# Moving one small product and its softmax away from the DMA that feeds it: a Fourier mix with eight experts on one core

## The chip, the cores and the metric

The kernel runs on one core of a Trainium2 chip. What is compared is the device time of one launch in microseconds (us). The engines are named as in the profile: PE is the matrix engine, PEld its weight loads, DVE the vector engine, ACT the scalar engine, POOL the general engine, and SP the engine whose queue issues most of the DMAs. Each works through its instructions in a fixed order and waits at an instruction until what it needs has been signalled.

## The reference, cut to what matters

The input has 8 batches of 2496 rows of 256 numbers. Each batch is transformed along its rows, mixed by two weight matrices in the frequency domain, cut by a soft threshold and transformed back. Each resulting row goes to one of 8 experts, and an expert keeps only its 80 rows of highest gate.

```python
X = np.fft.rfft(x, axis=1)
Yr = Xr @ w_r - Xi @ w_i + b_r
Yi = Xr @ w_i + Xi @ w_r + b_i
Yr = np.sign(Yr) * np.maximum(np.abs(Yr) - lam, 0.0)   # Yi alike
y = np.fft.irfft(Y, n=2496, axis=1)
...
logits = y @ w_gate                      # 19968 x 8
expert_idx = np.argmax(logits, axis=1)
probs = softmax(logits); gate_w = probs[n, expert_idx[n]]
for e in range(8):
    keep = the 80 rows of expert e with the highest gate_w
    out[keep] = gate_w[keep, None] * (np.maximum(y[keep] @ w1[e], 0) @ w2[e])
```

## The kernel before, in words

The main loop has 16 steps, two for each batch: step i works on half of batch i//2, and its first and last stages already serve the neighbouring steps. `stageA` (product at L296) transforms the input along one factor of the length and stores the result `zd` to memory; `loadZ` brings it back as `z`, half a step or more ahead of its use; `stageB` (product at L344, copies at L351 to L355) transforms along the other factor; `mixes` (products at L418, L460 to L470) mixes and thresholds; `stageTs` and `stageD` (L585 to L600) turn the result, and `stageHB` (L615, L640 to L652) makes the rows `hd` that the experts read later. Zero rows of the output (`out<-zero`, L268) are stored a few at a time all along.

A batch's gate is computed beside this. The logits come out of `stageD` in the small tile `Gs`. `stageE1a` sums them, `stageE1b` (L731 to L747) transforms them back along one factor and stores the result to memory as `gd` in two DMAs (L743, L744), then reads it back in the other order as `gr` in two DMAs (L747), which wait for the stores. `stageE2` is the product that turns the gate back along the second factor (L791) and behind it the softmax: ten instructions of DVE (L799 to L813) and one exponential of ACT (L801). `stageE3` transposes the result (L819) and copies it to `sall` (L824). From `sall` the best of each list are chosen: `level1(0)` and `level2` for the first four batches, as small operations that `doP` issues a few at a time (`pump`), the other four batches behind the loop.

Batch b's `stageE1b` is called in step 2b+3, its `stageE2` at the end of that step, and its `stageE3` in step 2b+4. All products write to tiles of a pool of four buffers in PSUM (`psum()`): a product waits until the engine that reads the buffer's former content is done with it. `stageE2` keeps its buffer from the product to the last of the ten instructions, which read and write in it. The order on each engine is made by a scheduler from the order of the calls, the dependences and its own costs; SP issues its DMAs in that order too, and a DMA that has to wait holds up those behind it.

The calls of step i that matter here, in the order in which they stand:

```python
doC(0, 0); doB(); doC(0, 1); doA(); doC(0, 2); doHB(); doB()
doP(); doW(...)
if pend3: stageE3(*pend3.pop())          # in step 10 then pump = level1(0), level2
pend = [(p[0], stageE1b(*p)) for p in pend]
...
if pend and not end:
    p = pend.pop(); sc = stageE2(*p)
doP(); doW(...)
```

Of the kernel before, what the change touches and what calls it, by code (L numbers as in the profile page):

```python
# [10 lines left out]
F32 = mybir.dt.float32  # L11
# [11 lines left out]
CAP = 80  # L23
# [109 lines left out]
def fourier_mix_then_moe(ctx, tc, x, w_r, w_i, b_r, b_i, wg, w1, w2, t1, t2, vq, v3, v0, v1f, vt, sg, cst, cb, out):  # L133
    nc = tc.nc
# [4 lines left out]
    ek = ctx.enter_context(tc.tile_pool(name="ek", bufs=1))  # L139
# [10 lines left out]
    gd = [dr.tile([39, 64, 8], F32, name=f"gd{b}") for b in range(B)]  # L150
# [219 lines left out]
    hops = []  # L370
# [36 lines left out]
    def doS():  # L407
        while totals:
            totals.pop(0)()
# [316 lines left out]
    def stageE1b(b, gp):  # L726
        pt = psum()

        for t, (tab, k) in enumerate(((vqs, 2), (vis, 8), (vqs, 14))):
            for v, h in ((0, 0), (0, 1), (1, 0)):  # L730
                nc.tensor.matmul(pt[:, 48 * t:48 * t + 48], tab[:, v], gp[:, h, k:k + 6, :], start=(v + h == 0), stop=(v == 1))  # L731
        special(pt[:64, 512:536], gp)
        gh = ek.tile([128, 21, 8], F32, name="gh", bufs=1)
        gu = ek.tile([128, 48], F32, name="gdif")
        sc = 2.0 / S / XS
        g = float(np.sqrt(0.75))
        at = lambda a: gh[:, 6 * a:6 * a + 6].rearrange("p k e -> p (k e)")
        nc.scalar.activation(at(0), pt[:, 0:48], AF.Copy, scale=sc)
        nc.scalar.activation(gh[:64, 18:21], pt[:64, 512:536].rearrange("p (a e) -> p a e", a=3), AF.Copy, scale=sc)
        nc.vector.scalar_tensor_tensor(gu, pt[:, 96:144], -1.5 * sc, at(0), op0=ALU.mult, op1=ALU.add)  # L740
        for a, f in ((1, g), (2, -g)):
            nc.vector.scalar_tensor_tensor(at(a), pt[:, 48:96], f * sc, gu, op0=ALU.mult, op1=ALU.add)
        nc.sync.dma_start(gd[b][0:21].rearrange("q n e -> n q e"), gh[0:64])  # L743
        nc.sync.dma_start(gd[b][21:39].rearrange("q n e -> n q e"), gh[64:128, 0:18])  # L744
        gr = ek.tile([78, 32, 8], F32, name="gr", bufs=1)
        for h in range(2):
            hops.append(nc.sync.dma_start(gr[39 * h:39 * h + 39], gd[b][:, 32 * h:32 * h + 32, :]))  # L747
        return gr

    def stageE1c(b, gp):  # L750

# [64 lines left out]
    def stageE3(b, sc):  # L816
        pt = psum()
        for h in range(2):
            nc.tensor.transpose(pt[:, 128 * h:128 * h + 78], sc[:, 4 * h:4 * h + 4].rearrange("p e n -> p (e n)"), ident[:78, :78])  # L819
        o, i = sall[:, :, b], pt[:, :256].rearrange("p (h f) -> p h f", h=2)[:, :, :78]  # L820
        if b >= B - 2:
            nc.vector.tensor_copy(o, i)
        else:
            nc.scalar.activation(o, i, AF.Copy)  # L824
# [84 lines left out]
    def doW(n=1):  # L909
        for _ in range(n):  # L910
            if wq:
                _, step, load = wq.pop(0)
                load()
                step()

                for w in wq[:2] if ahead else ():
                    w[2]()
# [54 lines left out]
    def level1(g):  # L972

        cv = None if g else const.tile([128, 2, 8], F32, name=f"cv{g}")
        ci = const.tile([128, 2, 8], U32, name=f"ci{g}")
        g0, n = 4 * g, 4
        if g:

            pt = psum()
            cv = pt[:, 512:528].rearrange("p (h r) -> p h r", h=2)  # L980
        for h in range(2):
            row = sall[:, h, g0:g0 + n].rearrange("p b r -> p (b r)")
            nc.vector.max(out=cv[:, h], in_=row)
            nc.vector.max_index(out=ci[:, h], in_max=cv[:, h], in_values=row)
        if g == 0:
            nc.sync.dma_start(cvd.rearrange("(h j) n r -> (j n) h r", h=2), cv)
        else:

            cm = VT[0].rearrange("p (h n r) -> p h n r", h=2, n=32)
            for h in range(2):  # L990
                vops.append(nc.vector.tensor_tensor(cm[:, h], mod32.unsqueeze(2).to_broadcast([128, 32, 8]), cv[:, h].unsqueeze(1).to_broadcast([128, 32, 8]), op=ALU.mult))
                hops.append(nc.tensor.matmul(pt[:8, 0:256], div32[:, h], cm[:, h].rearrange("p n r -> p (n r)"), start=(h == 0), stop=(h == 1)))
            Vs.append(pt[:8, 0:512])
        tok = const.tile([128, 2, 8, 4], I32, name="tokb" if g == 1 else "tok")
        nc.vector.memset(tok, 0)
        k = []
        new = lambda dt: const.tile([128, 2, 8], dt, name=f"tk{len(k)}", tag=f"tk{k.append(0) or len(k)}")
        inp = (lambda dt: pt[:, 512 + 16 * len(k):528 + 16 * len(k)].rearrange("p (q h r) -> p (q h) r", h=2, q=k.append(0) or 1)) if g else new
        k.append(0)
        if g:  # L1000
            tokens(new, inp, 8, tok, ci, g0, n, R1, 8, 0)
            return []
        return tokens(new, inp, 8, tok, ci, g0, n, 0, 8, 0, True)
# [409 lines left out]
    def doA(n=1):  # L1413
        for _ in range(n):
            if not Aq:
                if not xls:
                    preX()
                if xls:
                    (b, c), xt = xls.pop(0)
                    Aq.extend([(b, 2 * c, xt), (b, 2 * c + 1, xt)])  # L1420
            if Aq:
                stageA(*Aq.pop(0))
            if not Aq:
                preX()
# [3 lines left out]
    def doP(n=1):  # L1428
        for _ in range(n):
            if pump:  # L1430
                with tc.issue_after(dvs[-1].ins):
                    pump.pop(0)()

    def doHB(n=1):
        for _ in range(n):
            if HBq:
                stageHB(*HBq.pop(0))
# [56 lines left out]
    prev = None  # L1494
    Gs = None
    pend = []
    pend3 = []
    pend3 = []
    pump = []
    for i in range(len(steps)):  # L1500
        b, ch = steps[i]
        end = i + 1 == len(steps)
# [18 lines left out]
        def doB():  # L1521
            doS()
            if Bs:
                stageB(*Bs.pop(0))

        RR = {}

        parts = {}

        def doC(eh, k):  # L1530
            if k == 0:
                R = wkr.tile([128, 14 * 128], F32, name="R", bufs=2)
                RR[eh] = R.rearrange("p (c l k) -> p c l k", c=2, k=64) if b < B - 1 else R[:, :11 * 128].rearrange("p (l c k) -> p l c k", c=2, k=64)
                if b < B - 1:
                    parts[eh] = mixes(ch, XT, RR[eh], eh)
                    if i == 0 and eh == 0:
                        parts[eh][3](1)
                        parts[eh][3](0)
            fast = end or (i == 14 and eh == 1)
            if b < B - 1:  # L1540
                parts[eh][k]()
            else:
                stageC(ch, XT, RR[eh], eh, k, fast)
            doS()
            if k == (2 if b < B - 1 else 1) and not end:
                YT[eh] = wka.tile([128, 2, 11, 2, 64], F16, name="YT", bufs=3)
                if b < B - 1:
                    stageTs(ch, RR[eh], YT, eh)
                else:
                    stageT(ch, RR[eh], YT, eh, copy=False)  # L1550
                    if eh:
                        stageT2(ch, RR[1], YT, 1, False)
                        with tc.issue_after(yts[-1].ins):
                            stageT2(ch, RR[0], YT, 0, False)

        if end:
# [23 lines left out]
            with tc.high_priority():  # L1580
                gp = stageG0(b, prev[2])
                p = pend.pop()
# [7 lines left out]
        if i == 1:  # L1590
            doC(0, 0); doC(0, 1); doC(0, 2); doA()
        elif b < B - 1:
            doC(0, 0); doB(); doC(0, 1); doA(); doC(0, 2); doHB(); doB()
        else:
            doC(0, 0); doB(); doA(); doHB(); doB()
        if i == 13:
            late_load()
        doP(); doW({12: 1, 13: 1, 14: 1}.get(i, 1))
        if pend3:
            stageE3(*pend3.pop())  # L1600
            if i == 10:
                pump = level1(0)
                bg = level2("b", CAP, 8)
        if i == 11:
            late_ops, pump = pump, list(bg[3])
            while late_ops:
# [9 lines left out]
            doC(0, 1); doD(); doHB(); doB(); doD()  # L1616
        if i == 0:
            doA(3)
        doP(); doW({12: 1, 13: 1, 14: 1}.get(i, 1))
        if i > 0:  # L1620
            zfill()
# [9 lines left out]
        doP(); doW({12: 1, 13: 1, 14: 1}.get(i, 1))  # L1631
        if prev:
            HBq.extend((pb, YO, pch, x) for x in ((-1, 1, 0, 2) if pch == 0 else (1, 0, 2)))
        sc = None
        if i in (11, 12, 13):
            doP()
        if i > 0:
# [8 lines left out]
            flush()  # L1646
        if pend and not end:
            p = pend.pop()
            sc = stageE2(*p)
        doP(); doW({12: 1, 13: 1, 14: 1}.get(i, 1))  # L1650
        if sc is not None:
            pend3 = [(p[0], sc)]
        if i == 0:
            znext = loadZ(*steps[2])
            hold.clear()
# [38 lines left out]
    with tc.high_priority():  # L1694
        gr = back()
        sc = stageE2(b, gr, True)
# [101 lines left out]
```

## Time and profile before

| | us |
|---|---|
| median of 3 runs | 612.48 (609.36 to 618.34) |
| the profiled execution's own time | 609.48 |
| its span, first to last instruction | 607.7 |
| PE busy | 533.2 (88% of the span) |
| DVE busy | 403.9 (66%) |
| ACT busy | 352.5 (58%) |
| POOL busy | 377.5 (62%) |
| DMA, mean over the span | 219 GB/s |

The main loop takes about the first 490 us and the experts the rest. In a timeline a row gives the start, the duration and the instruction; brackets tell how long the engine had stood idle before it and what ended the wait. A matrix product of 32-bit numbers is recorded as several instructions. The clock of a stretch is the share of full speed that was granted to PE: 1.00 is 2.4 GHz, 0.50 is 1.2 GHz.

### The profile page before, as it was taken

The numbers are of one execution on the slowest core, as the hardware profiler recorded it, in microseconds if no ns is written. First come the engines' busy times: TensorE is split into PE (matmuls) and PEld (weight loads), VectorE is DVE, ScalarE is ACT, GpSimd is POOL, SyncE is SP. The second block draws the span as 40 slices with busy tenths as digits, with TensorE's granted clock in tenths as the row PEclk, the third lists the DMA queues.
The fourth block names the chain that finished last, engine by engine and source line by source line (L and its number), as shares of the span: only waits on it lengthen the run. The fifth ranks groups of instructions, "written<-read, shape, count | busy, mean of one in ns | idle before, by whom it ended". The sixth has DMA issues, their size and how long they took to land. (4 is left out here: it accounts for less than half of the span.)

```text
span 607.7 us, 11933 instructions
## 1 busy us (share of the span) xinstructions
PE 533.2 (88%) x4408; PEld 382.1 (63%) x4408; DVE 403.9 (66%) x829; ACT 352.5 (58%) x558; POOL 377.5 (62%) x306
## 2 busy tenths in 40 slices
PE   8978889999699999989997989997789997979592
PEld 3864566767376767766674657774666574539591
DVE  3145437767566888666765698897696777947650
ACT  1135557668366767765665557775675538543561
POOL 2012685778456777765687368698885259756671
PEclk9979999999799999999998899999799998998897
DMA  7898899798889878978898889798584545878730
GB/s 167 270 211 199 249 246 262 227 283 214 212 215 290 254 199 250 254 211 232 246 249 222 219 232 289 194 307 234 142 254 118 170 157 163 268 239 271 275 90 23
DMA packets 95869, 133.85 MB, mean 220 GB/s; under 512 B 27094, under 2 KB 78573, under 8 KB 94167
## 3 DMA queue, kind: packets, MB, share of 16 engines
q1 hardware_dynamic: 88124, 116.04, 69.1%
q0 software_dynamic: 2128, 9.25, 4.6%
q10 hardware_dynamic: 5553, 7.73, 4.4%
q8 instruction: 37, 0.61, 0.4%
q14 instruction: 27, 0.22, 0.1%
HBM read 70.36 MB, written 62.63 MB: 219 GB/s over the span
## 5 line engine op out<-in xcount | busy, mean ns | idle before, releaser
L418 PEld LDWEIGHTS <-WM 128*128 128x128 f16 x1008 | 99.1, 100 | 59.5 <-issue 14.4
L418 PE MATMUL ps<-XT,WM 128*128 128x337 f16 (+1 forms) x672 | 99.3, 297 | 7.4 <-DVE Gs L600 2.6
L529 POOL TENSOR_TENSOR YT<-R,YT 128x1408 f16<-128x1408 f32 (+1 forms) x28 | 73.4, 2620 | 46.5 <-ACT YT L528 46.5
L344 PE MATMUL ps<-t2s,z 128*128 128x128 f32 x640 | 86.6, 285 | 7.6 <-DMA z<-zd 4.7
L344 PEld LDWEIGHTS ps<-t2s,z 128*128 128x128 f32 x640 | 80.7, 199 | 11.6 <-DVE WM L213 4.0
L296 PE MATMUL ps<-xt,t1f 117*117 117x512 f32 (+1 forms) x170 | 80.2, 595 | 5.9 <-DMA xt<-in_x 2.3
L354 DVE TENSOR_TENSOR tp<-ps,tp 128x320 f32<-128x320 f32 (+2 forms) x56 | 27.3, 487 | 66.2 <-ACT XT L352 61.2
L470 POOL TENSOR_TENSOR R<-R,tp 128x674 f32<-128x674 f32 (+1 forms) x28 | 42.4, 1514 | 46.1 <-ACT R L468 46.1
L355 DVE TENSOR_TENSOR XT<-ps,XT 128x768 f16<-128x768 f32 (+1 forms) x64 | 52.1, 814 | 5.4 <-ACT XT L352 5.4
L640 PE MATMUL ps<-YO,vqs 128*128 128x512 f16 (+1 forms) x252 | 49.8, 339 | 3.4 <-DVE R L466 1.9
L597 DVE TENSOR_TENSOR YO<-ps,YO 128x768 f16<-128x768 f32 (+1 forms) x50 | 45.4, 908 | 7.1 <-ACT YO L596 6.9
L464 POOL TENSOR_TENSOR R<-R,sgs 128x576 f32<-128x576 f32 x28 | 36.2, 1294 | 19.6 <-DVE R L462 10.2
L296 PEld LDWEIGHTS ps<-xt,t1f 117*117 117x117 f32 (+1 forms) x170 | 27.9, 178 | 31.7 <-issue 22.2
L352 ACT ACTIVATE XT<-ps 128x768 f16<-128x768 f32 (+1 forms) x64 | 44.8, 700 | 2.8 <-PE ps L344 2.8
L585 PE MATMUL ps<-wgi,YT 128*128 128x144 f16 (+1 forms) x302 | 42.7, 227 | 2.1 <-DVE R L462 0.6
L596 ACT ACTIVATE YO<-ps 128x768 f16<-128x768 f32 (+1 forms) x50 | 38.4, 778 | 9.6 <-PE ps L586 9.3
L528 ACT ACTIVATE YT<-R 128x1408 f16<-128x1408 f32 (+1 forms) x28 | 35.6, 1270 | 13.2 <-POOL R L525 13.2
L640 PEld LDWEIGHTS <-vqs 128*128 128x128 f16 x252 | 25.2, 101 | 27.1 <-issue 10.6
L586 PE MATMUL ps<-wgi,YT 128*128 128x136 f16 (+1 forms) x302 | 41.5, 222 | 0.0
L351 ACT ACTIVATE tp<-ps 128x320 f32<-128x320 f32 (+2 forms) x56 | 24.3, 433 | 28.8 <-PE ps L344 24.8
L467 ACT ACTIVATE tp<-R,lams 128x674 f32<-128x674 f32 (+1 forms) x28 | 22.8, 815 | 19.4 <-DVE R L466 18.4
L311 ACT ACTIVATE zs<-ps 117x1024 f32<-117x1024 f32 (+1 forms) x23 | 21.8, 950 | 19.6 <-PE ps L296 15.2
(299 smaller groups left out, 1150.3 us busy)
## 6 DMA issues: line engine op xcount, KB each, us to landing
out<-zero SPq DMA_DIRECT2D x48, 384.0 KB
hd<-hs SPq DMA_DIRECT2D x96, 192.0 KB
zd<-zs SPq DMA_DIRECT2D x108, 156.0 KB
xt<-in_x SPq DMA_DIRECT2D x42, 312.0 KB
z<-zd SPq DMA_DIRECT2D x32, 320.0 KB
z<-zd SPq DMA_DIRECT2D x16, 384.0 KB
pair<-in_moe_w SPq DMA_DIRECT2D x11, 512.0 KB
z<-zd SPq DMA_DIRECT2D x16, 256.0 KB
```

Source lines behind the costliest of these rows:

```text
L296: nc.tensor.matmul(pt[:K, 512 * j:512 * j + 512], t1f[:K, :K], xv[:, 2 * j:2 * j + 2], start=True, stop=True)
L344: nc.tensor.matmul(o, z2[u][:, l, 128 * dh:128 * dh + 128], t2s[:, cl, :], start=True, stop=True)
L352: nc.scalar.activation(ov(0), pv, AF.Copy)
L355: nc.vector.tensor_tensor(ov(1), pv, ov(0), op=ALU.subtract)
L418: nc.tensor.matmul(pt[:, 512 * k:512 * k + n], WM[:, dh, m, wh, 128 * eh:128 * eh + 128], x(dh, xh)[:, c0 + n * k:c0 + n * k + n], start=( ...
L470: nc.gpsimd.tensor_tensor(fv(Rf), fv(Rf), fv(t), op=ALU.subtract)
L529: nc.gpsimd.tensor_tensor(yv(1), rv, yv(0), op=ALU.subtract)
L585: nc.tensor.matmul(pt[:, off:off + w], yt(0), wgi[:, eh, 0:w], start=True, stop=False)
L586: nc.tensor.matmul(pt[:, off:off + w - w % 128 // 2], yt(1), wgi[:, eh, 0:w - w % 128 // 2], start=False, stop=True)
L596: dev.append(nc.scalar.activation(yoh, yy, AF.Copy))
L597: dvs.append(nc.vector.tensor_tensor(yol, yy, yoh, op=ALU.subtract))
L640: nc.tensor.matmul(o, tab[:, v], yo(h), start=(i == 0), stop=(i == 2))
```

## The change

For batches 0 to 2 `stageE1b` now stores `gd` and hands back a function `turn`, which issues the two loads of `gr`; it is called at the end of the step, where `stageE2` was called before. `stageE2` itself is called in the next step: for batches 0 to 2 behind the first third, where `stageE3` stood, and for batch 3 (whose loads stay with `stageE1b`) behind the first `doB` of step 10. `stageE3` follows at the end of the step for batches 0 to 2 and in the middle of step 10 for batch 3; `level1(0)` and `level2` follow it there, and step 10 gets one more `doP`. Batches 4 to 7 keep their places.

```diff
-        gr = ek.tile([78, 32, 8], F32, name="gr", bufs=1)
-        for h in range(2):
-            hops.append(nc.sync.dma_start(gr[39 * h:39 * h + 39], gd[b][:, 32 * h:32 * h + 32, :]))
-        return gr
+
+        def turn():
+            gr = ek.tile([78, 32, 8], F32, name="gr", bufs=1)
+            for h in range(2):
+                hops.append(nc.sync.dma_start(gr[39 * h:39 * h + 39], gd[b][:, 32 * h:32 * h + 32, :]))
+            return gr
+        return turn if b < 3 else turn()
...
+        def doE(at):
+            if pend2 and at == (1 if i < 10 else 0 if i == 10 else 2):
+                p = pend2.pop()
+                pend3.append((p[0], stageE2(*p)))
+
+        def doE3():
+            nonlocal pump, bg
+            if pend3:
+                stageE3(*pend3.pop())
+                if i == 10:
+                    pump = level1(0)
+                    bg = level2("b", CAP, 8)
...
-            doC(0, 0); doB(); doC(0, 1); doA(); doC(0, 2); doHB(); doB()
+            doC(0, 0); doB(); doE(0); doC(0, 1); doA(); doC(0, 2); doHB(); doB()
...
-        if pend3:
-            stageE3(*pend3.pop())
-            if i == 10:
-                pump = level1(0)
-                bg = level2("b", CAP, 8)
+        doE(1)
+        if i > 10:
+            doE3()
...
+        if i == 10:
+            doE3()
...
             p = pend.pop()
-            sc = stageE2(*p)
+            pend2.append((p[0], p[1]() if p[0] < 3 else p[1]))
+        doE(2)
         doP(); doW({12: 1, 13: 1, 14: 1}.get(i, 1))
-        if sc is not None:
-            pend3 = [(p[0], sc)]
+        if i < 10:
+            doE3()
+        elif i == 10:
+            doP()
```

The scheduler moves few other instructions, and the same instructions stand in both programs. Lines of the changed kernel behind the first edit are higher: the product L791 is L794 there, the softmax L802 to L816, the transposes L822, the loads of `gr` L749.

On PE, the product of batch 0 stood behind the last product of `stageHB` for the first two classes (L615) and ahead of the next one (L640):

```order
L615 LDWEIGHTS v0s
L615 MATMUL ps<-YO,v0s 64x256
L791 MATMUL ps<-gr,v1fs 78x256
L640 LDWEIGHTS vqs
L640 MATMUL ps<-YO,vqs 128x512
```

It now stands behind the second `stageB` of the next step (`t2s`, `z`), ahead of the first `stageD` (`wgi`, `YT`):

```order
L344 MATMUL ps<-t2s,z_1606 128x128 x4
L794 MATMUL ps<-gr,v1fs 78x256
L585 LDWEIGHTS YT
L585 MATMUL ps<-wgi,YT 128x144
L586 LDWEIGHTS YT
```

That is the place where the transposes L819 stood; these now stand some 170 rows of PE further on, between two products of `stageHB`. For batch 3 the product stands behind the first `stageB` of the step instead.

On DVE, the softmax of batch 0 stood in one piece, ahead of the copies of the first `stageB` of the next step:

```order
L466 SCALAR_TENSOR_TENSOR R<-ps,thr,tp_135 128x576
L799 TENSOR_REDUCE gm<-ps 78x32
L800 TENSOR_TENSOR gdif<-ps,gm 78x256
L806 TENSOR_TENSOR ps<-ps,gm 78x256
L807 TENSOR_TENSOR ps<-ps,rank 78x256
L808 TENSOR_REDUCE gm<-ps 78x32
L809 TENSOR_TENSOR ps<-ps,gm 78x256
L810 TENSOR_REDUCE ps<-gex 78x32
L811 TENSOR_SCALAR gq<-ps 78x32
L812 RECIPROCAL gq<-gq 78x32
L813 TENSOR_TENSOR gr<-ps,gq 78x32x8
L354 TENSOR_TENSOR tp_136<-ps,tp_136 128x320
```

It now begins behind an L648 and is spread between the copies of the second `stageB`, of `stageHB` (L651, L652) and of two `stageD` (L597, L600), its last six in one piece ahead of an L460:

```order
L802 TENSOR_REDUCE gm<-ps 78x32
L354 TENSOR_TENSOR tp_136<-ps,tp_136 128x256
L355 TENSOR_TENSOR XT<-ps,XT 128x2x256
L803 TENSOR_TENSOR gdif<-ps,gm 78x256
L809 TENSOR_TENSOR ps<-ps,gm 78x256
L651 SCALAR_TENSOR_TENSOR hs<-ps,hs 128x768
L597 TENSOR_TENSOR YO<-ps,YO 128x768
L600 COPY Gs<-ps 128x96
L810 TENSOR_TENSOR ps<-ps,rank 78x256
L652 SCALAR_TENSOR_TENSOR hs<-ps,hs 128x768
```

All ten now come ahead of the L460 and of the copies (L354, L355) of the `stageB` that follows, which formerly came before that L460.

On SP, for batch 0, the loads of `gr` stood behind one half of a load of `z` and ahead of three stores of zeros:

```order
L744 DMA gd_94<-gh 64x18x8
L330 DMA z_1624<-zd_86 64x1024
L747 DMA gr<-gd_94 39x256 x2
L268 DMA out<-zero 96x4x256 x3
L332 DMA z_1624<-zd_86 64x1024
```

The three stores now go ahead of them, and both halves of `z` come behind:

```order
L744 DMA gd_94<-gh 64x18x8
L268 DMA out<-zero 96x4x256 x3
L749 DMA gr<-gd_94 39x256 x2
L330 DMA z_1606<-zd_86 64x1024
L332 DMA z_1606<-zd_86 64x1024
```

For batches 1 and 2 the same moves are made on all three engines; for batch 3 SP's order around `gr` is as before.

## Rows read from the trace of the kernel before

**Rows 1.** the page: busy us, share and instructions by engine

```profile
PE 533.2 (88%) x4408; PEld 382.1 (63%) x4408; DVE 403.9 (66%) x829; ACT 352.5 (58%) x558; POOL 377.5 (62%) x306
```

**Rows 2.** who waited for whom, whole run: engine, line, releaser, us, times, longest

```profile
PE ps L791 <- DMA gr<-gd: 12.0, 3, 5.2
...
PE ps L344 <- DMA z<-zd: 4.7, 3, 3.8
...
SPq L747 <- DMA gd<-gh: 15.8, 8, 4.3
```

**Rows 3.** timeline of PE: start us, us, line, tile, count [idle before <-releaser]

```profile
162.21 1.11 PE L791 MATMUL ps<-gr,v1fs 78*78 78x256 f32 x2 [5.23 <-DMA gr<-gd]
...
175.15 1.06 PE L344 MATMUL ps<-t2s,z 128*128 128x128 f32 x8
...
176.04 0.30 PE L819 MATMUL ps<-ident,gr 78*128 78x78 f32 x2
...
218.12 0.66 PE L791 MATMUL ps<-gr,v1fs 78*78 78x256 f32 x2
...
229.50 0.30 PE L819 MATMUL ps<-ident,gr 78*128 78x78 f32 x2
...
237.40 1.11 PE L344 MATMUL ps<-t2s,z 128*128 128x128 f32 x8
...
274.66 0.63 PE L791 MATMUL ps<-gr,v1fs 78*78 78x256 f32 x2 [3.37 <-DMA gr<-gd]
...
331.58 1.11 PE L791 MATMUL ps<-gr,v1fs 78*78 78x256 f32 x2 [3.43 <-DMA gr<-gd]
...
346.04 0.30 PE L819 MATMUL ps<-ident,gr 78*128 78x78 f32 x2
```

**Rows 4.** stretches: length, busy of PE PEld DVE ACT POOL, clock, DMA share, GB/s

```profile
229.50:237.40 7.90, 7.90 (x81) 6.41 (x79) 6.18 (x11) 5.79 (x11) 5.75 (x7) 1.00 0.82 213
...
162.20:167.20 5.00, 4.99 (x16) 2.59 (x17) 3.17 (x9) 1.11 (x2) 0.98 (x2) 0.50 0.97 267
331.60:337.10 5.50, 5.50 (x18) 2.86 (x19) 3.67 (x10) 1.11 (x2) 2.66 (x3) 0.50 0.97 273
157.00:162.20 5.20, 0.00 (x0) 0.02 (x1) 0.00 (x0) 1.61 (x4) 3.35 (x4) 0.83 0.62 114
271.30:274.70 3.40, 0.04 (x1) 0.07 (x2) 0.00 (x0) 1.61 (x4) 1.63 (x2) 1.00 0.27 75
...
382.00:414.00 32.00, 29.69 (x233) 21.64 (x231) 31.41 (x74) 25.49 (x39) 24.97 (x22) 1.00 0.93 270
```

**Rows 5.** timeline of SP's issues, batch 0

```profile
156.42 0.83 SPq L744 DMA_DIRECT2D gd<-gh  x1
157.36 0.68 SPq L330 DMA_DIRECT2D z<-zd  x1
159.94 0.73 SPq L747 DMA_DIRECT2D gr<-gd  x2
160.72 1.90 SPq L268 DMA_DIRECT2D out<-zero  x3
162.66 1.73 SPq L332 DMA_DIRECT2D z<-zd  x1
```

**Rows 6.** timeline of DVE, the softmax of batch 1

```profile
218.81 0.42 DVE L799 TENSOR_REDUCE gm<-ps 78x32 f32<-78x256 f32 x1 [0.47 <-PE ps L791]
219.27 0.42 DVE L800 TENSOR_TENSOR gdif<-ps,gm 78x256 f32<-78x256 f32 x1
219.61 0.42 DVE L806 TENSOR_TENSOR ps<-ps,gm 78x256 f32<-78x256 f32 x1
...
220.53 0.42 DVE L808 TENSOR_REDUCE gm<-ps 78x32 f32<-78x256 f32 x1
...
222.57 0.60 DVE L813 TENSOR_TENSOR gr<-ps,gq 78x256 f32<-78x256 f32 x1
```

**Rows 7.** timeline of DVE, small operations of the token list

```profile
390.32 0.15 DVE L940 SCALAR_TENSOR_TENSOR tk<-tk,tk 128x16 f32<-128x16 f32 x1
```

More of the change, by code (lines that the diff above doesn't have):

```diff
@@ L1496, in fourier_mix_then_moe @@
     pend = []
-    pend3 = []
+    pend2 = []
     pend3 = []
     pump = []
+    bg = None
     for i in range(len(steps)):
@@ L1592, in fourier_mix_then_moe @@
         elif b < B - 1:
-            doC(0, 0); doB(); doC(0, 1); doA(); doC(0, 2); doHB(); doB()
+            doC(0, 0); doB(); doE(0); doC(0, 1); doA(); doC(0, 2); doHB(); doB()
         else:
-            doC(0, 0); doB(); doA(); doHB(); doB()
+            doC(0, 0); doB(); doE(0); doA(); doHB(); doB()
         if i == 13:
@@ L1633, in fourier_mix_then_moe @@
             HBq.extend((pb, YO, pch, x) for x in ((-1, 1, 0, 2) if pch == 0 else (1, 0, 2)))
-        sc = None
         if i in (11, 12, 13):
```

## Prediction

> **What bounds the kernel now.** I read the page first. PE is busy 88% of the span and every other engine two thirds or less [rows 1], so in the main loop time is lost where PE stands still, or where it runs at half clock. Next comes the list of who waited for whom. Its longest entry for PE is the product that turns the gate back (L791), which waited 12.0 us in three waits for the loads of `gr`; SP, which issues them, in turn stood 15.8 us at L747 for the stores of `gd`, over eight waits [rows 2].
>
> The timeline of PE shows the three waits: 5.23 us for batch 0, 3.37 for batch 2, 3.43 for batch 3. For batch 1 there is none, since PE came late enough there [rows 3]. The table of stretches shows what went on around them. DVE did nothing at all in the two waits shown, and ACT and POOL finished what they had; nobody got ahead in them. And after the waits of batches 0 and 3 the granted clock is 0.50, PE's lower level of 1.2 GHz, for 5.0 and 5.5 us, with PE busy throughout; after the wait of batch 2 it stayed at 1.00 [rows 4].
>
> That a wait costs its full length is seen by going from L791 to the transposes L819: 11.38 us for batch 1, which had neither wait nor low clock, 13.83 for batch 0 and 14.46 for batch 3, which started late and then ran slowly [rows 3]. Nothing was caught up.
>
> **The change part by part.** The sum is made against the profiled execution, 609.48 us, of which 607.7 are span. The median of the runs is 3.0 us higher, 612.48.
>
> *The waits at L791.* For batches 0 to 2 the product now stands where L819 stood, 11 to 14 us later on PE [rows 3]. For batch 0, SP could issue the loads of `gr` at 159.94, as soon as the stores had landed, and the product started at 162.21, 1.5 us after they were issued [rows 3, 5]. Three stores of zeros (96 x 4 x 256 numbers of 4 bytes each) now go ahead of them: 1.18 MB, which at the 267 GB/s of the stretch behind the wait take 4.4 us [rows 4]. PE would reach the new place at 176.04 less the wait and the slow clock, near 168.3, some 6 us after the 162.2 at which `gr` was there before. That covers the 4.4, the more so as SP spends 1.90 us of its wait for `gd` on issuing the zeros [rows 5]. For batch 3 the loads keep their place and the product lets one product each of `stageHB`, `mixes` and `stageB` go first. The first two fill most of the stretch at half clock: 5.5 us less the 1.11 of L791 itself, so 2.2 at full clock; an L344 adds 1.1. These 3.3 us nearly cover the 3.43 [rows 3, 4]. The three waits go: 5.23 + 3.37 + 3.43 = 12.0 us.
>
> *The low clock.* Without waits of that length the clock has no reason here to fall. The 5.0 and 5.5 us of full work at 0.50 take half as long at 1.00: 5.25 us. The distances above give 13.83 + 14.46 less twice 11.38, so 5.5. I take 5.3.
>
> *The softmax on DVE, batches 0 to 2.* Its ten instructions took from 218.81 to 222.57 + 0.60, 4.36 us in one piece [rows 6]. In the old place they fill time in which DVE waits; in the new one DVE is wanted. From the transposes to the second L344 behind them, 229.5 to 237.4, DVE works 6.18 of 7.90 us, which leaves 1.72, and PE works all 7.90 [rows 4]. Of the ten, the first four now stand between instructions they don't depend on, and such a neighbour starts 0.34 us after the one ahead (L800 to L806) instead of about 0.46 (L799 to L800); the last six still follow one another and take 220.53 to 223.17, 2.64 us [rows 6]. So 4 x 0.34 + 2.64 = 4.0, less 1.72: 2.3 us for which DVE's copies come late. The copies free PSUM buffers, of which only three turn round while the softmax holds the fourth, and PE has nothing spare, so I count them as PE's wait: 3 x 2.3 = 6.9 us. The ends: nothing, if PE's products have that much slack to DVE; the whole 4.36 each, 13.1, if DVE's gaps can't be used. I take 6.9, since both the spacing and the gap are rows of this very place.
>
> The Trainium skill speaks against the interleaving ("VectorE: DVE Perf Modes", section "The DRAIN you can't avoid"): the next operation doesn't start before the pipeline of the one ahead is empty, and this can't be skipped. By it the ten would take 4.36 us wherever they stand, and the sum would be 3 x 0.36 = 1.1 higher. The trace differs a little: L806 starts 0.08 us before L800 ends [rows 6].
>
> *The old place.* It loses 4.36 us of DVE work per batch. For batch 1, where PE didn't wait, PE went on through it; so this gives nothing.
>
> *Batch 3's softmax* moves only some 4 us and mixes with the copies of step 10. Between nothing and the 2.3 of the others: 1.0.
>
> *The list of the first four batches.* Step 10 takes one more group of four small operations, which later steps don't have to take. Behind it DVE is the bound, busy 31.41 of 32.00 us [rows 4]. Four of them at 0.15 us [rows 7]: 0.6 us gained.
>
> *The rest.* The product itself (0.66 us), the transposes (0.30), the exponential and the copy to `sall` are only moved. SP's load of `z`, first half, moves behind the zeros and `gr`; its second half keeps its place behind them, so `z` is whole no later than before in the queue: nothing, or the third rival. POOL only exchanges two memsets with its neighbour: nothing.
>
> Sum: -12.0 - 5.3 + 6.9 + 1.0 - 0.6 = -10.0, so 609.5 - 10.0 = **599.5 us**.
>
> **The rivals.**
>
> *DVE's work is hidden.* For it: PE's product and DVE's copy are several buffers apart, and ACT does half of the reading. Against it: PE at 7.90 of 7.90 with a buffer fewer. Then 609.5 - 12.0 - 5.3 - 0.6 = 591.6. Chance 0.17.
>
> *The buffer held turns into a wait of the old size: slower.* The softmax keeps its PSUM buffer from the product to its last instruction, and that is now stretched over two `stageD` and a `stageHB`. If the second L344 behind it (237.40 in the case of batch 1 [rows 3]) can't start until then and PE stands for all 4.36 us in one piece, the clock falls too: a wait of 3.37 us left it at 1.00, one of 3.43 did not [rows 3, 4]. Each of three batches then costs 4.36 + 2.5, 20.6 in all, and the sum is -12.0 - 5.3 + 20.6 + 1.0 - 0.6 = +3.7: 613.2 us. It decides at a wait of about 3.4 us. Against it: the gap of 1.72 us, and that the four spread instructions leave PE work between. Chance 0.06. The Trainium skill has this case ("Perfetto Trace Analysis", section "Optimization Strategy"): the same gap again and again on the engine that should be full can mean that PSUM has no room for the next tile. No run here shows it at this place.
>
> *`z` comes late.* Without the wait PE reaches the second `stageB` of batch 0's step at 175.15 - 5.23 - 2.5 = 167.4 instead of 175.15 [rows 3]. The second half of `z` was issued until 164.39 [rows 5]; without the stop at `gr` that ends some 1 to 2 us sooner, and the zeros and `z` (1.70 MB, two halves of 64 x 1024 numbers) need 6.4 us at 267 GB/s, from about 158 to 159.9 on, so it would land at 164 to 166. That is a margin of one to three us, and PE has waited for `z` before, 4.7 us in three waits, the longest 3.8 [rows 2]. Three waits of the mean, 1.6 us, take 4.7 back: 604.2. At the longest, 11.4: 610.9. Chance 0.21.
>
> *The loop is bound by the DMA engines*, and the waits only moved along: they carry 0.82 to 0.97 of their time in full stretches [rows 4]. Then about 608. Against it: in the waits that share falls to 0.27 and 0.62, so there is room, and batch 1's steps run without a wait at that load. Chance 0.06.
>
> **How the numbers follow.** Forecast 0.50, hidden 0.17, `z` 0.21, DMA 0.06, buffer 0.06. The range 591 to 608 takes in the forecast with 0 to 4.36 us per batch less the outermost ends, most of the hidden case and most of the `z` case; the rest is about 0.2. Two per cent is about what a measurement of this kernel can tell from no change; below 612.48 that is 600.2, right beside the forecast. So faster by over 2%: the hidden case and somewhat over three fifths of the forecast's, 0.49. Slower by over 2%, above 624.7, is out of reach of every case worked out: 0.03. Within 2%: 0.48.
>
> **What would show it.** Right: no wait at the moved product in the list; the clock at 1.00 through batches 0 to 3; L791 to L791 of batches 1 and 2 some 55 to 56 us; new PE waits of 1 to 3 us per batch in the 8 us behind the product, released by DVE (L600, L355, L813). Wrong: none of these (591.6), or one of over 3.4 us with the clock at 0.50 behind it (613), or L344 waiting for `z` (604 and up). The whole is wrong if the runs of before had other waits than this profile shows, or if the experts, behind the loop, don't start earlier when the loop ends earlier.

## The result, and the profile after

| | before | after |
|---|---|---|
| median of 20 runs of each, first comparison (us) | 611.85 | 606.47 |
| ratio, 95% interval | | 0.986 (0.982 to 0.991) |
| second comparison: median of 17 and of 12 runs (us) | 610.14 | 606.28 |
| ratio, 95% interval | | 0.999 (0.994 to 1.004) |
| mean of all runs shown (92 and 32 runs, us) | 610.7 | 606.1 |

Runs of one kernel differ here by more than 1%, and the ratio is formed from the faster runs of each kernel, so that one quick run can move it; the means of all runs are therefore given too. They differ by 4.6 us, with two standard errors of 1.7; in the two comparisons by themselves it is 5.0 and 4.8 us, with two standard errors of 2.8 and 3.1. By these means the change makes the kernel faster by 0.8%, within the 2%; of the two ratios the first shows a gain and the second none. Forecast were 10.0 us and 599.5, with a range of 591 to 608.

The profiled execution took 609.62 us, as long as the one of before (609.48). The list of who waited for whom (engine, line, releaser; us, times, longest) answers to [rows 2]:

```profile
PE ps L418 <- DVE Gs L600: 6.4, 5, 1.6
PE ps L344 <- DMA z<-zd: 4.9, 2, 4.3
...
SPq L749 <- DMA gd<-gh: 7.9, 5, 3.7
```

The product (now L794) is no longer in it. At the head stands `mixes` (L418) waiting for DVE's copies L600: 6.4 us, 2.6 in the kernel before. Of the 4.9 us for `z`, 4.3 lie ahead of the loop's first gate, as all 4.7 did in the kernel before. SP stands half as long for `gd`. The timeline of PE (start, us; brackets: idle before) answers to [rows 3]:

```profile
170.88 1.13 PE L344 MATMUL ps<-t2s,z 128*128 128x128 f32 x8 [0.55 <-DMA z<-zd]
171.84 0.60 PE L794 MATMUL ps<-gr,v1fs 78*78 78x256 f32 x2
...
176.58 1.91 PE L418 MATMUL ps<-XSe,WM 128*128 128x337 f16 x12 [1.65 <-DVE Gs L600]
...
189.87 0.30 PE L822 MATMUL ps<-ident,gr 78*128 78x78 f32 x2
...
227.37 0.60 PE L794 MATMUL ps<-gr,v1fs 78*78 78x256 f32 x2
230.19 0.24 PE L585 MATMUL ps<-wgi,YT 128*128 128x144 f16 x1 [0.52 <-DVE XT L355]
232.42 1.76 PE L418 MATMUL ps<-XSe,WM 128*128 128x337 f16 x11 [1.32 <-DVE Gs L600]
...
283.50 0.60 PE L794 MATMUL ps<-gr,v1fs 78*78 78x256 f32 x2
288.24 1.91 PE L418 MATMUL ps<-XSe,WM 128*128 128x337 f16 x12 [1.65 <-DVE Gs L600]
...
331.97 0.60 PE L794 MATMUL ps<-gr,v1fs 78*78 78x256 f32 x2
...
344.19 1.03 PE L418 MATMUL ps<-XSe,WM 128*128 128x337 f16 x6 [0.95 <-ACT sall L827]
```

The product never waits. Five microseconds behind it PE does, 1.3 to 1.7 us per batch and released by DVE: the wait that the prediction named. From product to product it is 55.5 and 56.1 us. In the stretches (length, busy of PE PEld DVE ACT POOL, clock, DMA share, GB/s) the one around batch 1's new place and the one behind batch 3's product answer to [rows 4]:

```profile
226.40:234.30 7.90, 6.06 (x57) 4.53 (x55) 7.50 (x14) 4.74 (x8) 6.28 (x9) 1.00 0.83 222
332.00:337.00 5.00, 5.00 (x28) 2.87 (x27) 4.36 (x9) 3.43 (x5) 3.65 (x4) 1.00 0.90 257
```

DVE works 7.50 of 7.90 us where it had worked 6.18; the clock stays at 1.00. On DVE the softmax of batch 0 is spread over 8.8 us (compare [rows 6]: 4.36), since copies stand in between:

```profile
172.47 0.42 DVE L802 TENSOR_REDUCE gm<-ps 78x32 f32<-78x256 f32 x1 [1.16 <-PE ps L794]
...
174.22 0.42 DVE L809 TENSOR_TENSOR ps<-ps,gm 78x256 f32<-78x256 f32 x1
174.55 0.94 DVE L651 SCALAR_TENSOR_TENSOR hs<-ps,hs 128x768 f32<-128x768 f32 x1
...
178.66 0.41 DVE L811 TENSOR_REDUCE gm<-ps 78x32 f32<-78x256 f32 x1
...
180.64 0.61 DVE L816 TENSOR_TENSOR gr<-ps,gq 78x256 f32<-78x256 f32 x1
```

A ruler for the whole loop is the first product of `stageE1b` in each batch, L731 in both kernels: 141.49 for batch 0 and 477.30 for batch 6 before, 144.73 and 472.86 after.

| L731 to L731 (us) | batch 0 | 1 | 2 | 3 | 4 | 5 | sum |
|---|---|---|---|---|---|---|---|
| before, the profile of the prediction | 60.6 | 53.7 | 56.3 | 62.4 | 53.0 | 49.9 | 335.8 |
| before, second profile | 59.4 | 53.7 | 53.8 | 59.6 | 55.7 | 46.4 | 328.6 |
| before, third profile | 55.0 | 55.1 | 60.2 | 55.8 | 56.2 | 47.5 | 329.8 |
| after | 56.0 | 56.4 | 55.2 | 56.6 | 55.1 | 48.8 | 328.1 |
| after, second profile | 55.2 | 56.4 | 55.2 | 56.6 | 52.8 | 49.4 | 325.8 |

Against the profile of the prediction the loop became 7.7 us shorter; against the mean of three profiles of before (331.4) the mean of two of after (326.9) is 4.5 shorter, about as in the runs. The second and third profiles were taken last; they are the key to the size.

### The profile page after: what moved, and what is told of

The parts are those of the page before. It is cut to its first block, busy times and chain, and to the rows that moved or that the text cites. A ratio compares the mean times of both kernels' runs of the same rounds, so it can differ in the third digit from the quotient of the medians.

```text
span 607.8 us, 11926 instructions
## 1 busy us (share of the span) xinstructions
PE 531.9 (88%) x4408; PEld 379.3 (62%) x4408; DVE 402.5 (66%) x829; ACT 352.1 (58%) x558; POOL 377.2 (62%) x306
## 2 busy tenths in 40 slices
DMA packets 95870, 133.85 MB, mean 220 GB/s; under 512 B 27095, under 2 KB 78574, under 8 KB 94168
## 5 line engine op out<-in xcount | busy, mean ns | idle before, releaser
L418 PEld LDWEIGHTS <-WM 128*128 128x128 f16 x1008 | 98.1, 99 | 64.0 <-issue 18.6
L418 PE MATMUL ps<-XT,WM 128*128 128x337 f16 (+1 forms) x672 | 99.0, 297 | 6.8 <-ACT XT L352 1.8
L529 POOL TENSOR_TENSOR YT<-R,YT 128x1408 f16<-128x1408 f32 (+1 forms) x28 | 73.4, 2620 | 33.0 <-ACT YT L528 33.0
L344 PE MATMUL ps<-t2s,z 128*128 128x128 f32 x640 | 85.0, 282 | 9.8 <-DMA z<-zd 4.9
L296 PE MATMUL ps<-xt,t1f 117*117 117x512 f32 (+1 forms) x170 | 82.5, 608 | 8.1 <-DMA xt<-in_x 4.3
L344 PEld LDWEIGHTS ps<-t2s,z 128*128 128x128 f32 x640 | 79.2, 196 | 14.6 <-issue 4.7
L354 DVE TENSOR_TENSOR tp<-ps,tp 128x320 f32<-128x320 f32 (+2 forms) x56 | 27.3, 487 | 72.4 <-ACT XT L352 65.6
L355 DVE TENSOR_TENSOR XT<-ps,XT 128x768 f16<-128x768 f32 (+1 forms) x64 | 51.9, 812 | 4.7 <-ACT XT L352 4.7
L640 PE MATMUL ps<-YO,vqs 128*128 128x512 f16 (+1 forms) x252 | 48.5, 330 | 2.6 <-DVE R L466 0.9
L296 PEld LDWEIGHTS ps<-xt,t1f 117*117 117x117 f32 (+1 forms) x170 | 28.2, 181 | 35.9 <-issue 24.2
L597 DVE TENSOR_TENSOR YO<-ps,YO 128x768 f16<-128x768 f32 (+1 forms) x50 | 45.3, 905 | 5.0 <-ACT YO L596 4.8
L640 PEld LDWEIGHTS <-vqs 128*128 128x128 f16 x252 | 24.2, 99 | 25.4 <-issue 8.0
L443 ACT ACTIVATE tp<-ps 128x674 f32<-128x674 f32 (+1 forms) x28 | 19.4, 692 | 26.8 <-PE ps L418 26.5
```

Source lines behind the costliest of these rows:

```text
L296: nc.tensor.matmul(pt[:K, 512 * j:512 * j + 512], t1f[:K, :K], xv[:, 2 * j:2 * j + 2], start=True, stop=True)
L344: nc.tensor.matmul(o, z2[u][:, l, 128 * dh:128 * dh + 128], t2s[:, cl, :], start=True, stop=True)
L355: nc.vector.tensor_tensor(ov(1), pv, ov(0), op=ALU.subtract)
L418: nc.tensor.matmul(pt[:, 512 * k:512 * k + n], WM[:, dh, m, wh, 128 * eh:128 * eh + 128], x(dh, xh)[:, c0 + n * k:c0 + n * k + n], start=( ...
L529: nc.gpsimd.tensor_tensor(yv(1), rv, yv(0), op=ALU.subtract)
L597: dvs.append(nc.vector.tensor_tensor(yol, yy, yoh, op=ALU.subtract))
```

## The experiments

Ratios are to the kernel before, with 95% intervals; medians are of all runs.

**The move without batch 3** (e4_no3). Batch 3's product, softmax, transposes and list stay where they were.

```diff
-            if pend2 and at == (1 if i < 10 else 0 if i == 10 else 2):
+            if pend2 and at == (1 if i < 9 else 2):
...
```

> The move for batches 0 to 2 alone; batch 3's product, softmax, transposes and list stand as before. Theory (the time comes batch by batch from the waits and from the low clock behind them): the stretch of batch 3 gains no longer its 5.8 us, so about 2 to 3 us below the kernel before (ratio 0.995 to 0.997), a wait of about 3 us at the product of batch 3 with the clock at 0.50 behind it. Rival (the clock falls for another reason, or the stretch of batch 3 profits from the earlier ones): the ratio stays near the change's 0.986.

Ratio 0.991 (0.986 to 0.996), median 605.32 against 610.79. Batch 3's wait was gone although its product had not moved, which the theory of this run had not expected; one of the three profiles of before, though, has no wait there either. Its store of `gd` was issued at 316.56, 1.2 us after the DVE instruction that completes `gh` (L742) had ended at 315.35; in the first profile of before that took from 315.91 to 324.76, 8.9 us.

The three profiles of before show that the wait is decided on SP. In all twelve cases, four batches in each profile, PE reached the product, its wait taken off, 11.6 to 12.2 us behind the end of L742. Where SP issued the store 2.6, 3.3 or 5.1 us behind it, PE did not wait; in the nine cases with 5.5 to 10.1 us it did. Batch 1 of the first profile, which did not wait, had 5.1:

```profile
205.64 0.31 DVE L742 SCALAR_TENSOR_TENSOR gh<-ps,gdif 128x48 f32<-128x48 f32 x2
...
211.03 0.60 SPq L743 DMA_DIRECT2D gd<-gh  x1
```

**Product and softmax behind the first `stageB`** (e2_first), and **the loads of `gr` at once** (e3_loads):

```diff
-            if pend2 and at == (1 if i < 10 else 0 if i == 10 else 2):
+            if pend2 and at == (0 if i <= 10 else 2):
...
-        return turn if b < 3 else turn()
+        return turn()
...
```

(the second kernel lacks the first two of these lines).

> As the change, but batches 0 to 2 have product and softmax where the change puts batch 3's, behind the first stage B of the step, and their loads of gr are issued at once. Theory (the softmax costs 2 to 3 us per batch where DVE is full, and less where it has gaps): no wait at the product, batch 1's stretch about 54 to 55 us instead of 56.5, together 3 to 6 us below the change, ratio to the kernel before 0.977 to 0.981. Rival (the place costs nothing, the rest is bound elsewhere): as the change, 0.986. Second rival (the product comes too early again): waits at it of 1 to 3 us, ratio 0.988 to 0.995.

> As the change, but the loads of gr of batches 0 to 2 are issued at once, in SP's order of before; the product stays late. Theory (the order on SP costs and gives nothing): as the change, ratio to the kernel before 0.983 to 0.990. Rival (holding the loads back behind the zeros is what spares SP its wait and keeps z early): 2 to 5 us slower than the change, and SP stands again some 12 to 15 us for the stores of gd.

The first gave 0.999 (0.994 to 1.003), 608.97: the product waited again, 3.8 us in two waits, the longest 2.8. That is the second rival, a little dearer than it said. The second gave 0.999 (0.994 to 1.003), 609.22, with the loop at 328.1, as with the change. The change itself, run again but on another chip, gave 606.28 and the same ratio. The medians speak for the rival here, and SP stood 13.6 us for `gd` in place of 7.9, as the rival said; the loops of the profiles speak against it. Whether the order of the loads is worth some 3 us stays open.

**Early stores** (e1_early). The kernel before, with `stageE1b` of batches 0 to 3 called a third of a step earlier; product and softmax in their old places.

```diff
-            doC(0, 0); doB(); doC(0, 1); doA(); doC(0, 2); doHB(); doB()
+            doC(0, 0); doB()
+            if i < 10:
+                pend = [(p[0], stageE1b(*p)) for p in pend]
+            doC(0, 1); doA(); doC(0, 2); doHB(); doB()
...
-        pend = [(p[0], stageE1b(*p)) for p in pend]
+        if i >= 10:
+            pend = [(p[0], stageE1b(*p)) for p in pend]
```

> The kernel before, with the store and the loads of batches 0 to 3 about a third of a step earlier and the product and softmax in their old places: it takes the wait away without moving the softmax. Theory (waits and low clock are the price, the softmax in its old place costs nothing): waits at the product gone, clock 1.00, 12 + 5 us less, ratio 0.970 to 0.975. Rival (the DMA engines bound the loop, a wait moves to the next load): ratio 0.99 to 1.00, with a new wait for xt or z of some 3 us per batch.

Ratio 0.979 (0.973 to 0.985), median 595.24 in six runs: the best version of all, three times the gain of the change, by a few lines, if a little less than was expected. No product waited, and the rows of DVE, SP and PE for batch 0 show why:

```profile
138.23 0.31 DVE L742 SCALAR_TENSOR_TENSOR gh<-ps,gdif 128x48 f32<-128x48 f32 x2
...
142.71 0.63 SPq L743 DMA_DIRECT2D gd<-gh  x1
...
147.83 0.72 SPq L747 DMA_DIRECT2D gr<-gd  x2
...
157.43 0.66 PE L791 MATMUL ps<-gr,v1fs 78*78 78x256 f32 x2
```

`gr` is asked for 9.6 us ahead of the product. In the kernel before SP issued the store long after the data were there, behind stores of `hd` and `zd`:

```profile
145.03 0.31 DVE L742 SCALAR_TENSOR_TENSOR gh<-ps,gdif 128x48 f32<-128x48 f32 x2
...
150.20 1.99 SPq L319 DMA_DIRECT2D zd<-zs  x3
152.29 3.03 SPq L631 DMA_DIRECT2D hd<-hs  x4
155.44 0.63 SPq L743 DMA_DIRECT2D gd<-gh  x1
```

That is 10.1 us from the end of L742; for batches 1 to 3 it was 5.1, 6.9 and 8.9. With early stores it is 4.2, 1.6, 1.1 and 0.1 for batches 0 to 3. From the store to the product in [rows 3] only 6.8 us pass. With early stores PE is busy 122.4 of 125 us at full clock:

```profile
130.00:255.00 125.00, 122.38 (x972) 89.22 (x971) 92.65 (x152) 87.73 (x138) 91.42 (x75) 1.00 0.91 256
```

**Early stores and late places** (e5_late), **the same without batch 3** (e8_late3). Since no product waits with early stores, adding the late places prices these alone. The edit of e5_late on top of early stores is the change's `doE` and `doE3`, with the loads at once; e8_late3 has e4_no3's edit as well.

```diff
-            doC(0, 0); doB()
+            doC(0, 0); doB(); doE(0)
             if i < 10:
                 pend = [(p[0], stageE1b(*p)) for p in pend]
...
+        doE(1)
+        if i > 10:
+            doE3()
```

> The kernel with early stores (ratio 0.979 to the kernel before, no wait at the product) and on top of it the late places of the change for product, softmax, transposes and list of batches 0 to 3: what it loses against that kernel is the price of the late places alone. Theory (2.3 us per batch where DVE is full, 1 to 3 for batch 3 and its list): 7 to 9 us slower than the early stores alone, ratio to the kernel before 0.990 to 0.994, the loop's batches 0 to 2 some 56 us each instead of 53.5. Rival (the late places cost nothing, and the change lost its gain to SP and the DMA): 0.977 to 0.981.

> As the kernel with early stores and late places, but batch 3's product, softmax, transposes and list stand where they stood before the change. Theory (batch 3's part of the move, with no wait to take away, costs 1 to 3 us): 1 to 3 us faster than with batch 3's move, ratio 0.986 to 0.990. Rival (batch 3's part is worth its 0.4 us or nothing): the same as with it.

With the late places: 0.991 (0.988 to 0.995), median 605.00, which is 10 us slower than early stores alone; without batch 3: 0.988 (0.983 to 0.992), 602.91. L731 to L731 of batches 0 to 2 took 56.0, 57.2 and 56.0 us against 53.8, 53.4 and 53.6: 8.4 us for the three. (Over the whole loop the two profiles lie 6.1 us apart, since batch 4, whose time moves about in the kernel before too, took 51.3 us against 55.9.) Batch 3's part is 3.0 us by the means of the runs (two standard errors 2.5), and 0.7 by L731 of batch 6 in the two profiles (467.3 and 466.6).

**Eleven more instructions of DVE** (e6_dve), on tiles in SBUF. This is the kernel with early stores, the softmax in its old place, and behind it work whose result is not used.

```diff
+            if i < 10:
+                again(p[0])     # reduce, subtract, compare, multiply ... on gdif and gex, 78x256
```

> The kernel with early stores, product and softmax in their old places, and eleven more instructions of DVE of the softmax's sizes behind the transposes of batches 0 to 2, on tiles in SBUF, whose result nobody reads. Theory (what the late softmax costs is DVE's time, some 4.3 us per batch less the gap of 1.7): 6 to 8 us slower than the early stores alone, ratio 0.988 to 0.993. Rival (it costs through the PSUM buffer that it holds, which this one does not): 0 to 2 us slower, 0.979 to 0.983.

Ratio 0.992 (0.989 to 0.996), median 606.07: 11 us slower than early stores alone, and batches 0 to 2 at 56.9, 57.8 and 58.4. No buffer in PSUM is held here, so the rival's 0 to 2 us falls: DVE's time is enough to cost that much. The instructions were dearer than meant, though (last section), 7.3 to 8.7 us per batch in place of the softmax's 4.4, and 4.1 us per batch showed. So it is not shown that the held buffer adds nothing in the change. The waits between 130 and 305 us with early stores, with the late places, and with the added work:

```profile
PE ps L418 <- DVE Gs L600: 0.6, 1, 0.6
```

```profile
PE ps L418 <- DVE Gs L600: 4.6, 3, 1.6
```

```profile
PE ps L418 <- DVE Gs L600: 7.8, 3, 2.7
```

It is the same wait each time: PE's `mixes` for the buffer that DVE's copy of `stageD` reads. But it is not the whole price. The stretches of batches 0 to 2 with early stores, with the late places and with the added work (length, busy of PE first):

```profile
134.51:295.25 160.74, 156.98 (x1218) 112.87 (x1215) 121.27 (x197) 113.35 (x178) 115.63 (x96) 1.00 0.91 260
...
134.62:303.78 169.16, 158.02 (x1217) 113.06 (x1215) 120.45 (x197) 113.20 (x178) 117.47 (x98) 1.00 0.89 254
...
133.81:306.94 173.13, 161.25 (x1218) 114.21 (x1216) 141.80 (x230) 113.32 (x178) 116.81 (x96) 0.98 0.86 247
```

PE stood still for 3.8, 11.1 and 11.9 us. So with the late places the named wait brings 4.0 of the 8.4 us; the rest is mostly waits of under 1 us each, for ACT (L461) and for other copies of DVE (L313, L355) among others. With the added work two of the waits, 2.33 and 2.74 us long, had the low clock behind them, in batches 1 and 2:

```profile
239.40:242.80 3.40, 3.40 (x10) 1.77 (x9) 3.19 (x5) 0.79 (x2) 2.51 (x2) 0.50 1.03 318
297.40:300.80 3.40, 3.40 (x12) 1.85 (x11) 3.40 (x6) 0.68 (x1) 1.85 (x2) 0.50 0.95 321
```

PE is busy throughout these two stretches and would have needed half as long at 1.00, so that, as an estimate, 3.4 of that run's 12.4 us are the clock's.

**The wait filled** (e7_warm, e7b_warm). The kernel before, with products that nobody reads ahead of the gate's.

```diff
+            if b in (0, 2, 3):
+                w = WM[:, 0, 0].rearrange("p a b -> p (a b)")
+                for _ in range(18 if b == 0 else 12):
+                    nc.tensor.matmul(pt[:, 512:1024], w[:, 0:128], w, start=True, stop=True)
```

> The kernel before, with products of 128 x 512 on weights, whose result nobody reads, ahead of the gate's product of batches 0 (18 of them), 2 and 3 (12 each): PE works through most of the wait, the wait stays. Theory (the wait costs its own length and, apart from that, 5 us through the low clock behind it): the clock stays at 1.00 behind the product, 4 to 6 us less, ratio 0.990 to 0.994, the waits at the product still 12 us with the filling counted in. Rival (the low clock costs nothing, since the DMA sets the pace there): 0.998 to 1.003.

> The kernel with the filled waits once more, for a second profile: its first was the fastest of its twelve runs, with the loop at 328 us and no low clock behind the product, while the twelve runs together were no faster than the kernel before. Theory (filling gives the low clock back, and the others of its runs lost it elsewhere or in longer waits): the clock again at 1.00 behind the three products, the loop 327 to 331 us. Rival (the filling does not hold the clock, the first profile was chance): 0.50 behind a product, the loop 334 us or more.

The first profile shows the filling, the product and the clock behind it:

```profile
155.59 4.06 PE L794 MATMUL ps<-WM 128*128 128x512 f16 x18
159.49 0.60 PE L795 MATMUL ps<-gr,v1fs 78*78 78x256 f32 x2
```

```profile
159.50:164.50 5.00, 5.00 (x37) 3.66 (x36) 4.03 (x10) 3.33 (x6) 3.44 (x4) 1.00 0.96 276
```

In both profiles the clock is 1.00 behind all three products, and batch 0 takes 56.7 us. The second profile of before, with the low clock and a wait of 3.60 us there, took 59.4; here the product came 15.5 us behind L742, some 3.8 later than PE without a wait, so filling gives about 3 us back. All the same the runs gave 1.003 (0.998 to 1.007), median 613.81, which is what the rival said, and the loop of the second profile is 334.6. Where the wait was short the filling itself costs: batch 2 took 57.2 and 58.3 against 53.8 in the second profile of before. So it is shown, at six products in two profiles, that the low clock comes of PE standing still there, but not that filling pays; why its runs as a whole were no faster is not settled.

**The change and the kernel before once more** (a2_after, b2_before, b3_before).

> The changed kernel once more, unaltered, on the chip of the experiments and with a second profile. Theory (the order of the loads on SP is worth nothing, and the ratio of 0.999 of the kernel with loads at once is spread): ratio 0.988 to 0.995, the loop from the first gate transform to the last again 328 us. Rival (the loads behind the zeros are worth 0.5 to 1 per cent): ratio 0.983 to 0.988.

> The kernel before once more, for a second profile. Theory (the three waits and the low clock behind two of them belong to the kernel): waits at the product of 10 to 14 us in three, the clock at 0.50 behind one or two of them, the loop 334 to 338 us. Rival (they belong to that one execution): other waits, the loop 330 us or less.

> The kernel before, for a third profile, after the first had waited 12.0 us at the gate's product (loop 335.8 us) and the second 6.6 us (loop 328.6 us). Theory (the size of the waits differs from one execution to the next, and the first was one of the long ones): 5 to 10 us in two or three waits, the loop 328 to 334 us. Rival (12 us is the rule, and the second was the exception): 10 to 14 us, the loop 334 to 338 us.

The waits at the product in the second and the third profile of before:

```profile
PE ps L791 <- DMA gr<-gd: 6.6, 3, 3.6
```

```profile
PE ps L791 <- DMA gr<-gd: 7.8, 3, 4.3
```

So 12.0 us was the longest of three, and the mean is 8.8; the second profile came out as its rival said, the third as its theory. It moves about, too: batch 0 waited 5.23, 3.60 and 2.12 us, batch 1 nothing, nothing and 1.33, batch 2 3.37, 0.86 and 4.34, batch 3 3.43, 2.11 and nothing. The loop of a2_after, 325.8 us, is near what its theory said; its ratio of 0.999 lies outside both of its ranges. The low clock moves with it; behind batch 0's product in the second profile, and behind those of batches 0 and 2 in the third:

```profile
159.10:164.10 5.00, 4.95 (x16) 2.61 (x17) 3.14 (x9) 1.11 (x2) 2.56 (x3) 0.50 0.96 263
```

```profile
155.90:160.90 5.00, 5.00 (x36) 3.67 (x37) 4.02 (x10) 2.33 (x5) 3.90 (x4) 1.00 0.97 273
...
268.10:273.10 5.00, 4.95 (x16) 2.60 (x17) 3.13 (x9) 1.11 (x2) 1.91 (x2) 0.50 0.94 261
```

## Why the prediction was right in kind and too large in size

- **The time.** 606.5 us lies inside the range of 591 to 608, 1.5 us from its upper end. The ends of the range were made from the price of the softmax and from the rivals, not from the spread of the waits, which, with the low clock behind them, took away about half of the forecast gain; that the range held is partly luck.
- **The waits, -12.0.** They went, at all places, as forecast. But the size came from one execution, and the other two show 6.6 and 7.8 us; the mean is 8.8. This is the term that was mis-sized, and the prediction had named it as what would make the whole wrong. Its reason why batch 1 did not wait, that PE came late enough, does not hold: PE came 12.2 us behind L742, as in batch 3, which waited; SP's store was earlier.
- **The low clock, -5.3.** Right in kind: 1.00 through batches 0 to 3 after the change. In the three profiles it cost 5.3 us, some 4.2 (a whole stretch at 0.50 and one of 5.0 us at 0.66 in the mean, shown in the last section) and 2.5: 4.0 in the mean.
- **The softmax at the busy place, +6.9.** Forecast 2.3 per batch, measured 2.8 on top of early stores (8.4 for three). In the change itself it is about 2.5 (7.5): batches 0 to 2 took 167.7 and 166.9 us, against 159.5, 159.9 and 160.0 in the profiles of before less their waits and their low clock. So 1.6 to 1.9 of the 4.36 us were hidden, close to the gap of 1.72, and this term was nearly right. The wait came where it was named, in PE 5 us behind the product, from L600, but it is about half of the price. The spacing was read rightly too: in the changed kernel L651 starts 0.33 us behind L809, before L809 has ended. The section of the Trainium skill that the prediction sets against this ("VectorE: DVE Perf Modes", "The DRAIN you can't avoid") itself says that a next operation which is not held starts earlier, which the prediction leaves out.
- **Batch 3, +1.0, and the list, -0.6.** Together forecast at 0.4; measured as 0.7 in profiles and 3.0 in runs. The interval behind it, batch 4, took 55.1 and 52.8, against 53.0 to 56.2 before. The 0.6 cannot be told from that spread.
- **Sum by the measured terms:** -8.8 - 4.0 + 8.4 + 0.7 = -3.7, against -4.5 in the loops and -4.6 in the runs. With 7.5 for the softmax it is -4.6, but the 7.5 comes from the same profiles as the loops, so that this agreement is partly built in.
- **The rivals.** That DVE's work is hidden is refuted by e5_late. The held buffer did not turn into a wait of the old size: the longest is 1.65 us, and the added work costs without any buffer. Its threshold of 3.4 us for the clock was no rule either (last section). `z` was late by 0.55 us, once in the two profiles of after, and the waits for `z` that gave this rival its price all lay ahead of the loop's first gate. That the DMA engines bound the loop is refuted by early stores, which take 15 us off with the same 133.85 MB.
- **What the prediction did not see.** It took the wait for one of DMA latency, to be covered by going later. [rows 5] shows SP's stores, but their time was not compared with the DVE instruction that makes the data: 10.1 us lay there. Going earlier with the store keeps the softmax where DVE is idle and takes the whole gain.
- **Start and end.** Both profiles of after begin the loop's first gate 3 to 6 us later than those of before (144.7 and 144.6 against 138.2 to 141.5), though the order of instructions there is the same. At about 50 us `stageB` waited 2.2 and 2.5 us for a DMA in them, and the four products L296 behind took 3.8 us instead of 2.0; in the three of before that wait is 0.5 us or less. It looks like chance: e2_first, e3_loads, e4_no3 and e7_warm, with the same order up to there, begin at 139.8, 141.9, 143.2 and 140.2, and e7_warm waited 2.2 us at that place with 2.0 us for the products behind. But through it the loop ends no earlier in the profiles of after (L731 of batch 6 at 471.6 in the mean, against 471.3 before), and both of these executions lie 3 us above the median of their kernel. So the gain of the whole rests on the runs. An earlier end of the loop did carry to the end: with early stores L731 of batch 6 comes at 461.1 and the span ends at 595.5.

## What to carry to other kernels

Where an engine waits for a DMA, look first at when that DMA was issued and when its data were ready: if its queue is late, move the issue forward before moving the consumer back. Work moved out of an idle stretch of a second engine into a busy one has a price even off the critical engine; here over half of its length came back as time of PE. And a wait read from one execution is a sample: take two or three profiles before its size enters a sum.

## What the runs showed of the hardware

Instructions of DVE that read two tiles of SBUF could last until one of POOL that ran beside them ended. In e6_dve L827 took 2.24 us and ended 0.3 us behind POOL's L529; L826, of the same size, had begun 0.15 us before L529 and took 0.41:

```profile
177.55 0.41 DVE L826 TENSOR_TENSOR gdif<-gex,gm 78x256 f32<-78x256 f32 x1
178.71 2.24 DVE L827 TENSOR_TENSOR gex<-gdif,rank 78x256 f32<-78x256 f32 x1
...
177.70 2.97 POOL L529 TENSOR_TENSOR YT<-R,YT 128x1408 f16<-128x1408 f32 x1 [1.49 <-ACT YT L528]
```

The Trainium skill has this ("GPSIMD Engine Reference", section "1. Specifications"): POOL shares its way to SBUF with DVE, and they get in each other's way when a DVE instruction has two inputs in SBUF. The trace agrees for L827; L826 had already begun, and took its 0.41. The softmax's own instructions of 78x256, none of which reads two tiles of SBUF, took 0.39 to 0.43 us throughout, the last of them 0.57 to 0.61. The same is seen at the end of the kernel. Behind the loop, in the profile of after, two instructions of some 0.2 us ended only with POOL's (528.20 and 528.19, 530.40 and 530.33):

```profile
526.67 1.53 DVE L1084 TENSOR_TENSOR fl<-gh,fl 8x1 f32<-8x1 f32 x1
...
528.68 1.72 DVE L1090 TENSOR_TENSOR t0b<-t0b,gh 8x64 f32<-8x64 f32 x1
...
526.06 2.13 POOL L899 TENSOR_TENSOR pair<-pair,pair 128x1024 bf16<-128x1024 f32 x1 [2.95 <-ACT pair L878]
528.15 2.18 POOL L899 TENSOR_TENSOR pair<-wt,pair 128x1024 bf16<-128x1024 f32 x1
```

In the first profile of before POOL stood idle at that place, from 526.8 to 530.82, and they took 0.15 and 0.20 us. From L731 of batch 6 to the end it was 130.4 us there, and 131.7 to 139.4 in the other profiles; how much of that these instructions make is not shown.

The clock: a wait of 2.12 us (batch 0, third profile of before) left it at 1.00, one of 2.11 (batch 3, second profile) had a stretch at 0.66 in the mean behind it, and 3.37 (batch 2, first profile) left it at 1.00 again. In e4_no3 a wait of only 1.32 us for L600, in batch 1, had 0.50 behind it, while the same wait left it at 1.00 in both profiles of after. The stretches behind the 2.11 and the 1.32 us:

```profile
325.10:330.10 5.00, 5.00 (x22) 2.86 (x23) 3.59 (x10) 1.11 (x2) 3.91 (x4) 0.66 0.98 278
...
230.30:233.70 3.40, 3.40 (x14) 2.09 (x13) 3.26 (x9) 0.17 (x1) 2.40 (x3) 0.50 0.78 197
```

The length of a wait alone does not tell.
